# Score products and products with v on one ring of PSUM banks, with joined visits and two casts on other engines

## The chip, the cores and the metric

The program runs on one core of a Trainium2 chip. The metric is the device time of one execution in microseconds. A core has TensorE (PE, matrix products), VectorE (DVE), ScalarE (ACT), GpSimd (POOL) and SyncE (SP, which here only issues DMAs). Each engine works through its own queue in order; they meet through semaphores. TensorE writes its products to PSUM, eight banks of 2 KB per partition.

## The reference

Attention over 4 batches, 12 heads, 448 positions and 64 dimensions a head, with the heads mixed before and after the softmax, and two feed-forward layers behind it:

```python
scores = scale * np.matmul(q, k.transpose(0, 1, 3, 2))
scores = np.einsum('bhij,hg->bgij', scores, w_pre)
scores = scores - np.max(scores, axis=-1, keepdims=True)
attn = np.exp(scores)
attn = attn / (np.sum(attn, axis=-1, keepdims=True) + 1e-09)
attn = np.einsum('bhij,hg->bgij', attn, w_post)
out = np.matmul(attn, v)
# x: (1792, 768), all heads of a position in one row
h = x @ w_in;  x = (h * np.cos(h)) @ w_out
g = x @ w_gate;  y = (g / (1 + np.exp(-g)) * (x @ w_val)) @ w_out2
```

## The kernel before, in words

**Chunks and blocks.** The query positions of a batch are cut into four chunks of 12, 12, 11 and 10 blocks (`CH`); a block is ten positions with all twelve heads, 120 rows. 180 blocks in all, numbered through. The main loop (L438) runs over steps i, and in step i the stages of several blocks are issued: the score mix `premix` of block i, `rowmax` and `expo` of block i - 1, `den` of i - 2, `rec` and `norm_hi` of i - 3, `norm_lo` of i - 4, the post mix `post` of i - 6, `at_hi` and `at_lo` of i - 7 (lags, L336). What a step issues, and in which order, is set by the tuple `order` (L389): each engine's queue is that order restricted to its own work.

**A block's path.** `premix` (L220, TensorE, tile psm) mixes the heads of the scores x by `w_pre` into one of two banks. `rowmax` (L225, VectorE) takes the row maximum, `expo` (L233, ScalarE) the exponential and its row sum; both read the bank, which is free after `expo`. `den` and `rec` (L240, L244, VectorE) form the reciprocal. `norm_hi` (L249, GpSimd) and `norm_lo` (L256, VectorE) write the normalised rows as a sum of two fp16 parts. `post` (L269 to L271, twelve small products, TensorE, tile psa, two banks) mixes the heads again and transposes; `at_hi` (L282, ScalarE) and `at_lo` (L290, VectorE) write the result as two fp16 parts and free the bank.

**Score products.** The scores of a chunk are made while the chunk before is worked on. `qk` (L195, TensorE, tile pss) handles one head pair m of six: six products, three for each of two heads, with keys and queries as sums of a high and a low part. It takes two banks of the pool ps_s, which has two. `spread` (L211, ScalarE) copies a head's bank to a staging tile s (five of them) and issues, on SyncE's queue, the DMA that spreads it over x (L213). `QK_STEPS` gives the step of each head pair after the chunk's start; its two spreads stand one step later. The first mix of the next chunk needs all twelve spreads.

**Products with v.** `pv` (L302, TensorE, tile psv) handles one head pair: 24 products of 64 columns of weights. Three pairs share one bank of the pool ps_v, which also has two banks; `pv_out` (L319 ScalarE, L320 VectorE) empties it one step after the third. `PV_STEPS` gives the steps, counted from the end of the chunk, by the length of the chunk that follows. The small products of `pow2_b` and `w_sum_all` take banks of ps_v as well.

**Loads.** `dma_q` (L128) loads a chunk's queries seven steps before the chunk in front of theirs starts; `hi_q` (L132, VectorE, two halves) casts the high part and `lo_q` (L136, GpSimd) subtracts. `dma_k`, `hi_k` (L113, ScalarE) and `lo_k` (L117, GpSimd) do the same for the next batch's keys during the third chunk. `dma_v` (L140) loads a quarter of v, 112 positions; `split_v` scales it in place (L176, ScalarE), casts the high part (L179, VectorE) and subtracts in two halves (L182, GpSimd), over four steps that start two steps behind the load. Raw tiles of v have three buffers; all loads stand in SyncE's queue.

**Behind the attention.** The feed-forward part starts with the last chunk's early pieces and has its own loop; its lines are L732 to L734 (first products), L777 to L779 (second ones).

Of the kernel before, what the change touches and what calls it, by code (L numbers as in the profile page):

```python
# [7 lines left out]
F32 = mybir.dt.float32  # L8
# [9 lines left out]
SB = bass.MemoryType.SB  # L18
# [5 lines left out]
COFF = (0, 120, 240, 350)  # L24
CREAL = (120, 120, 110, 98)
FIRST = 4
QK_STEPS = {12: (0, 1, 3, 5, 7, 8), 11: (0, 4, 5, 6, 7, 8), 10: (0, 2, 3, 5, 6, 7)}
PV_STEPS = {11: (13, 13, 13, 15, 17, 17), 12: (11, 11, 11, 13, 15, 17), 10: (10, 10, 10, 14, 16, 16)}
SM = 1.0 / 8.0
INV2PI = 0.15915494309189535  # L30
TWOPI = 6.28318500518799
# [9 lines left out]
def attention(ctx, tc, qT, kT, vN, mix, xs, ff):  # L41
    nc = tc.nc
    scores = ExitStack()
# [7 lines left out]
    p_k = pool("a_k", 7, SB, scores, "right")  # L51
    p_kr = pool("a_kr", 3, SB, scores, "right")
    p_q = pool("a_q", 3, SB, scores, "right")
    p_s = pool("a_s", 5, SB, scores, "right")
    ps_s = pool("ps_s", 2, PSUM, scores, "right")
    p_vr = pool("a_vr", 3, SB, scores, "right")
    p_x = ff.p_x
# [8 lines left out]
    mixed = ExitStack()  # L66
    ps_m = pool("ps_m", 2, PSUM, mixed)

    ones = const.tile([128, 128], F32, name="ones")
    nc.vector.memset(ones, 1.0)  # L70
    nc.vector.tensor_copy(ff.ones, ones)
# [7 lines left out]
        return diag  # L79

    def pow2_b(diag, n, name):
        ps = ps_v.tile([128, 512], F32, tag="pv", name=f"psp_{name}")
        nc.tensor.matmul(ps[:, :n], ones[:n, :], diag[:n, :n], start=True, stop=True)
        return ps

# [10 lines left out]
        nc.vector.tensor_scalar(p[:, 1:2], p[:, 1:2], 8.0, None, op0=ALU.mult)  # L96
        return p

    ff.ps_sum = lambda name: ps_v.tile([128, 512], F32, tag="pv", name=name)
    ktiles, qtiles, vtiles, vscale = {}, {}, {}, {}  # L100
    raws = {}

# [24 lines left out]
        for s in parts:  # L127
            nc.sync.dma_start(raws["q", b, c][:, s], src[:, s])  # L128

    def hi_q(b, c, e, copy=nc.vector.tensor_copy):  # L130
        s = slice(3 * e, 3 * e + 3)
        copy(qtiles[b, c][0][:, s], raws["q", b, c][:, s])  # L132

# [36 lines left out]
    def split_v(b, jc, part):  # L170

        r = raws["v", "r", b, jc]
        rv = r.rearrange("p (m e d) -> p m e d", e=2, d=D)
        by = vscale[b][:112, 1:2]
        if part == 0:
            nc.scalar.activation(r, r, AF.Copy, scale=by)  # L176
        elif part == 1:
            t = vtiles[b, jc] = p_v.tile([112, 6, 2, 2, D], F16, tag="v", name=f"v_{b}_{jc}")
            nc.vector.tensor_copy(t[:, :, :, 0], rv)  # L179
        else:  # L180
            t, m = vtiles[b, jc], slice(3 * part - 6, 3 * part - 3)
            nc.gpsimd.tensor_tensor(t[:, m, :, 1], rv[:, m], t[:, m, :, 0], op=ALU.subtract)  # L182

    X, SP, SMALL, PM, E, EHL, PA, AT, PV = ({} for _ in range(9))

    def qk(b, c, m, places=((ps_s, "s"),)):

        n = 10 * CH[c]
        for e in range(2):
            pool, tag = places[(2 * m + e) % len(places)]  # L190
            SP[b, c, 2 * m + e] = pool.tile([128, 512], F32, tag=tag, name=f"pss_{b}_{c}_{2 * m + e}")
        for i, (zq, zk) in enumerate(((0, 0), (1, 0), (0, 1))):
            for e in range(2):
                r = slice(64 * e, 64 * e + 64)
                nc.tensor.matmul(  # L195
                    SP[b, c, 2 * m + e][:n, :S], qtiles[b, c][zq][r, m, :n], ktiles[b, m][zk][r],
                    start=(i == 0), stop=(i == 2),
                )
# [93 lines left out]
    def pv(b, c, m):  # L292


        n = 10 * CH[c]
        if m % 3 == 0:
            PV[b, c, m // 3] = ps_v.tile([128, 4, 128], F32, tag="pv", name=f"psv_{b}_{c}_{m}")
        ps = PV[b, c, m // 3]
        prods = [(jc, zv, za) for jc in range(4) for zv, za in ((0, 0), (0, 1), (1, 0))]
        for i, (jc, zv, za) in enumerate(prods):  # L300
            for e in range(2):
                nc.tensor.matmul(  # L302
                    ps[64 * e:64 * e + 64, m % 3, :n].rearrange("p (k i) -> p k i", i=10),
                    vtiles[b, jc][:, m, e, zv], AT[b, c][za][:, :, jc * H + 2 * m + e],
                    start=(i == 0), stop=(i == len(prods) - 1),
                )
# [24 lines left out]
    def at(i, fn, *a):  # L331
        plan.setdefault((i, fn.__name__), []).append((fn, a))

    first = {bc: blocks.index((*bc, 0)) for bc in chunks}
    for i, blk in enumerate(blocks):
        for fn, lag in ((premix, 0), (rowmax, 1), (expo, 1), (den, 2), (rec, 3), (norm_hi, 3),  # L336
                        (norm_lo, 4), (post, 6), (at_hi, 7), (at_lo, 7)):
            at(i + lag, fn, *blk)
    for ci, (b, c) in enumerate(chunks):
        n, s0 = CH[c], first[b, c]  # L340
        if ci + 1 < len(chunks):
            nb, ncn = chunks[ci + 1]
            for m in range(6):
                i = s0 + QK_STEPS[n][m]
                at(i, qk, nb, ncn, m)
                for e in range(2):
                    at(i + 1, spread, nb, ncn, 2 * m + e)
            if ci:
                at(s0 - 7, dma_q, nb, ncn)
                for e in range(2):  # L350
                    at(s0 - 2 + e, hi_q, nb, ncn, e)
                    at(s0 - 1 + e, lo_q, nb, ncn, e)
        if c == 2 and b + 1 < B:
            for m in range(6):
                i = s0 + 1 + 14 * m // 6
                at(i - 1, dma_k, b + 1, m)
                at(i + 2, hi_k, b + 1, m)
                at(i + 3, lo_k, b + 1, m)
        if c == 0:
            if b == 0:  # L360
                for part in range(3):
                    at(4 + part, scale_v, 0, part)
            if b + 1 < B:
                for part in range(3):
                    at(first[b, 3] + 7 + part, scale_v, b + 1, part)
            for jc in range(4):
                if b == 0:
                    if jc == 3:
                        at(1, dma_v, 0, jc, "m")
                    at(jc, max_v, 0, jc)  # L370
                v0 = s0 + 4 * jc + 5
                at(v0, dma_v, b, jc, "r")
                for part in range(4):
                    at(v0 + 2 + part, split_v, b, jc, part)
                if b + 1 < B:
                    i = first[b, 3]
                    at(i + jc, dma_v, b + 1, jc, "m")
                    at(i + jc + 2, max_v, b + 1, jc)
# [6 lines left out]

    for i, fn, *a in ff.early_plan(first[B - 1, 3]):
        at(i, fn, *a)

    order = (  # L389
        "rec", "pv_out", "pv", "post", "at_hi", "l1_part", "rowmax", "dma_v", "at_lo", "w_sum",  # L390
        "w_sum_all", "w_unit", "w_bits", "hidden", "den", "max_v", "scale_v", "hi_k", "dma_q",
        "lo_q", "spread", "split_v", "dma_k", "w_dma", "x_load", "load_next", "new_scale", "hi_q",
        "w_max", "w_shift", "w_split", "expo", "norm_hi", "premix", "qk", "lo_k", "norm_lo",
    )


    with tc.manual_schedule():
        vec, act, pl = nc.vector, nc.scalar, nc.gpsimd
# [39 lines left out]
        for i in range(-1, NB + 24):  # L438
            if i == first[B - 1, 3]:
                scores.close()  # L440
                ff.open_early()
            if i == NB + 1:
                mixed.close()
                ff.open_ps()
            for kind in order:
                for fn, a in plan.pop((i, kind), []):
                    fn(*a)
    assert not plan
# [529 lines left out]
```

## Time and profile before

| | |
|---|---|
| three runs | 1461.84, 1462.12, 1464.26 us; median 1462.12 |
| the profiled execution | 1462.24 us; span of its instructions 1460.4 us |
| TensorE | busy 1408.3 us, 96% of the span |
| VectorE | busy 1068.1 us, 73% |
| ScalarE | busy 646.3 us, 44% |
| GpSimd | busy 494.4 us, 34% |
| mean granted TensorE clock | 0.987 |

In the chain that ended last, followed back from the last instruction, TensorE has 76% of the span, VectorE 15%, ScalarE 4%, DMA transfers 3%. The busy shares are means over two very different parts, attention and feed-forward, so they are read by stretches. Matrix products are pipelined and overlap in the records: for TensorE the distance from one start to the next says more than an instruction's own duration, and in the rows below an "x6" is the first start and the whole length of six products.

### The profile page before, as it was taken

Reading aid. Unit: us, or ns where it says so; the run is one execution under the profiler, and the core shown is the slowest. Engines: PE = TensorE matmul, PEld = TensorE weight load, DVE = VectorE, ACT = ScalarE, POOL = GpSimd, SP = SyncE. Lnnn points to the kernel's source line nnn. Section 1 sums busy time; section 2 is a strip of 40 time slices with the busy share of each in tenths; the row PEclk is TensorE's granted clock in tenths of the full one; section 3 lists DMA queues with packets and bytes.
Section 4 is the critical chain, followed back from the end, with each engine's and each line's share of the span. In section 5 each row is a group of like instructions: output and inputs, shape, how many; then the busy total and the mean of one; then the engine's idle time right before and its main releaser. Section 6 shows DMA issues by size and latency. Waiting matters only on the chain.

```text
span 1460.4 us, 27063 instructions
## 1 busy us (share of the span) xinstructions
PE 1408.3 (96%) x10330; PEld 940.7 (64%) x10330; DVE 1068.1 (73%) x2310; ACT 646.3 (44%) x1374; POOL 494.4 (34%) x522
## 2 busy tenths in 40 slices
PE   6999999999999899999999999989999999999999
PEld 2556666656665566767676766656666666666666
DVE  5888989888988667878888878786355656565523
ACT  3777877877865353333333332444422223222210
POOL 2553553553532233323333332332223223222210
PEclk9999999999999999999999999999999999999999
DMA  6555555555546112121212221021112212211013
GB/s 203 147 155 152 154 157 157 149 156 149 156 140 226 44 55 77 54 66 54 77 54 66 65 65 44 22 65 55 55 44 66 66 44 69 62 55 33 1 38 114
DMA packets 102264, 131.77 MB, mean 90 GB/s; under 512 B 29848, under 2 KB 88696, under 8 KB 102136
## 3 DMA queue, kind: packets, MB, share of 16 engines
q1 hardware_dynamic: 101296, 128.77, 29.8%
q8 instruction: 81, 1.33, 0.4%
q10 hardware_dynamic: 840, 1.29, 0.3%
q14 instruction: 47, 0.39, 0.1%
HBM read 80.95 MB, written 10.37 MB: 63 GB/s over the span
## 4 chain that ended last, share of the span: by engine, by line
PE 76%; DVE 15%; ACT 4%; DMA 3%; issue 2%; SPq 0%; POOL 0%; ACTq 0%; DVEq 0%; POOLq 0%
PE ph L732 10%; PE ph L734 10%; PE ph L733 10%; PE psm L220 9%; PE py L777 7%; PE py L778 7%; PE py L779 7%; PE pss L195 5%; PE psv L302 4%; PE psa L269 3%; PE psa L270 2%; PE psa L271 2%; DVE acc L783 2%; DVE r L750 2%; DVE r L753 2%
## 5 line engine op out<-in xcount | busy, mean ns | idle before, releaser
L732 PE MATMUL ph<-x,h_i 128*128 128x448 f16 x960 | 339.4, 354 | 0.0
L733 PE MATMUL ph<-x,h_i 128*128 128x448 f16 x960 | 338.9, 353 | 0.0
L734 PE MATMUL ph<-x,l_i 128*128 128x448 f16 x960 | 338.9, 353 | 0.0
L762 POOL TENSOR_TENSOR gl<-r,gh 128x448 fp32r<-128x448 f32 x112 | 131.6, 1175 | 411.4 <-ACT gh L761 406.1
L777 PE MATMUL py<-gh,h_o 128*128 128x448 f32 x672 | 257.8, 384 | 11.5 <-DVE acc L783 6.2
L778 PE MATMUL py<-gl,h_o 128*128 128x448 f32 x672 | 245.5, 365 | 0.0
L779 PE MATMUL py<-gh,l_o 128*128 128x448 f32 x672 | 245.2, 365 | 0.1
L783 DVE TENSOR_TENSOR acc<-py,acc 128x448 f32<-128x448 f32 x288 | 174.4, 619 | 64.2 <-PE py L779 60.3
L220 PE MATMUL psm<-x,wpre_sb 120*120 120x448 f32 x360 | 181.1, 586 | 17.8 <-DMA x<-s 7.1
L249 POOL TENSOR_SCALAR eh<-e,sm 120x448 f16<-120x448 f32 x180 | 115.0, 639 | 183.8 <-DVE sm L244 113.9
L732 PEld LDWEIGHTS <-h_i 128*128 128x128 f16 x960 | 93.9, 98 | 92.4 <-issue 10.6
L777 PEld LDWEIGHTS py<-gh,h_o 128*128 128x128 f32 x672 | 127.3, 189 | 37.1 <-DVE acc L783 16.9
L734 PEld LDWEIGHTS <-l_i 128*128 128x128 f16 x960 | 94.0, 98 | 87.9 <-issue 0.4
L733 PEld LDWEIGHTS <-h_i 128*128 128x128 f16 x960 | 94.2, 98 | 82.0 <-issue 0.2
L225 DVE TENSOR_REDUCE sm<-psm 120x1 f32<-120x448 f32 x180 | 110.6, 615 | 41.7 <-PE psm L220 40.2
L233 ACT ACTIVATE e<-psm,sm 120x448 f32<-120x448 f32 x180 | 115.7, 643 | 56.9 <-DVE sm L225 55.1
L606 POOL TENSOR_TENSOR l_i<-f_i,h_i 128x384 f16<-128x384 f32 x80 | 81.3, 1016 | 174.9 <-ACT h_i L605 174.7
L760 DVE SCALAR_TENSOR_TENSOR r<-ph,by_i,r 128x448 f32<-128x448 f32 x48 | 32.8, 684 | 146.5 <-PE ph L734 115.8
L269 PE MATMUL psa<-wpost,eh 120*112 120x120 f16 x720 | 131.8, 226 | 4.9 <-DVE at L290 2.3
L779 PEld LDWEIGHTS py<-gh,l_o 128*128 128x128 f32 x672 | 127.0, 189 | 10.3 <-POOL l_o L606 1.3
L778 PEld LDWEIGHTS py<-gl,h_o 128*128 128x128 f32 x672 | 127.4, 190 | 7.5
L761 ACT CAST gh<-r 128x448 fp32r<-128x448 f32 x112 | 63.5, 567 | 155.0 <-DVE r L760 117.8
(105 smaller groups left out, 2451.3 us busy)
## 6 DMA issues: line engine op xcount, KB each, us to landing
r_o<-in_w_out SPq DMA_DIRECT2D x56, 384.0 KB
x<-s SPq DMA_DIRECT2D x84, 210.0 KB
r_i<-in_w_in SPq DMA_DIRECT2D x32, 384.0 KB
x<-s SPq DMA_DIRECT2D x48, 192.5 KB
r_i<-in_w_gate SPq DMA_DIRECT2D x24, 384.0 KB
r_i<-in_w_val SPq DMA_DIRECT2D x24, 384.0 KB
x<-s SPq DMA_DIRECT2D x48, 175.0 KB
qr<-in_qT SPq DMA_DIRECT2D x15, 360.0 KB
```

Of the source, the lines that this page charges most:

```text
L220: nc.tensor.matmul(ps[:120, :S], wpre_sb, X[b, c][:120, k], start=True, stop=True)
L233: nc.scalar.activation(e, PM.pop((b, c, k))[:120, :S], AF.Exp, bias=sm[:, 0:1], scale=1.0, accum_out=sm[:, 1:2])
L249: nc.gpsimd.tensor_scalar(eh, E[b, c, k], sm[:, 3:4], 1.0, op0=ALU.mult, op1=ALU.mult)
L269: nc.tensor.matmul(o, eh[:, j], wpost_sb[0], start=True, stop=False)
L732: nc.tensor.matmul(ps, wh, xh, start=(kk == 0), stop=False)
L733: nc.tensor.matmul(ps, wh, xl, start=False, stop=False)
L734: nc.tensor.matmul(ps, wl, xh, start=False, stop=(kk == 5))
L762: nc.gpsimd.tensor_tensor(gl, r, f(gh), op=ALU.subtract)
L777: nc.tensor.matmul(ps, wh, gh[:, e], start=(e == 0), stop=False)
L778: nc.tensor.matmul(ps, wh, gl[:, e], start=False, stop=False)
L779: nc.tensor.matmul(ps, wl, gh[:, e], start=False, stop=(e == 1))
L783: nc.vector.tensor_tensor(acc, ps, acc, op=ALU.add)
```

## The change

The constants: `QK_STEPS`, `PV_STEPS`, the steps of the loads and the order within a step are new; lags stand in a tuple, where `rec` moves from lag 3 to lag 2.

```diff
-QK_STEPS = {12: (0, 1, 3, 5, 7, 8), 11: (0, 4, 5, 6, 7, 8), 10: (0, 2, 3, 5, 6, 7)}
-PV_STEPS = {11: (13, 13, 13, 15, 17, 17), 12: (11, 11, 11, 13, 15, 17), 10: (10, 10, 10, 14, 16, 16)}
+LAGS = (0, 1, 1, 2, 2, 3, 4, 6, 7, 7)
+QK_STEPS = {12: (1, 1, 3, 3, 7, 7), 11: (1, 1, 3, 3, 7, 8), 10: (1, 1, 3, 3, 5, 6)}
+PV_STEPS = {12: (9, 9, 11, 17, 17, 17), 11: (10, 10, 10, 15, 15, 15), 10: (7, 9, 9, 15, 15, 15)}
+SECOND = 2
+Q_STEPS = (-11, -5, 0)
+K_STEPS = (3, 4, 6, 8, 10, 12)
+V_STEPS = (0, 3, 6, 9)
+SPLIT_STEPS = (3, 5, 6, 7)
+ORDER = (
+    "at_hi", "l1_part", "rowmax", "post", "dma_v", "lo_q", "premix", "den", "dma_k", "w_dma",
+    "x_load", "load_next", "new_scale", "split_v", "hi_k", "spread", "norm_hi", "max_v", "at_lo",
+    "w_sum", "w_sum_all", "w_unit", "w_bits", "hidden", "lo_k", "qk", "hi_q", "pv", "scale_v",
+    "rec", "norm_lo", "pv_out", "w_max", "w_shift", "w_split", "expo", "dma_q",
+)
-    p_s = pool("a_s", 5, SB, scores, "right")
+    p_s = pool("a_s", 6, SB, scores, "right")
+    banks = []
+
+    def bank(name):
+
+        second = len(banks) % 4 > 1 or "closed" in banks
+        banks.append(name)
+        pool, tag = (ps_v, "pv") if second else (ps_s, "s")
+        return pool.tile([128, 512], F32, tag=tag, name=name)
-        ps = ps_v.tile([128, 512], F32, tag="pv", name=f"psp_{name}")
+        ps = bank(f"psp_{name}")
-    ff.ps_sum = lambda name: ps_v.tile([128, 512], F32, tag="pv", name=name)
+    ff.ps_sum = bank
-    def hi_q(b, c, e, copy=nc.vector.tensor_copy):
+    def hi_q(b, c, e, copy=nc.scalar.copy):
-            nc.vector.tensor_copy(t[:, :, :, 0], rv)
+            nc.gpsimd.tensor_copy(t[:, :, :, 0], rv)
-    def qk(b, c, m, places=((ps_s, "s"),)):
+    def qk(b, c, m, places=()):
...
+                SP[b, c, 2 * m + e] = bank(name)
-            PV[b, c, m // 3] = ps_v.tile([128, 4, 128], F32, tag="pv", name=f"psv_{b}_{c}_{m}")
+            PV[b, c, m // 3] = bank(f"psv_{b}_{c}_{m}").rearrange("p (g i) -> p g i", g=4)
+                late = m and QK_STEPS[n][m - 1] == QK_STEPS[n][m]
                 for e in range(2):
-                    at(i + 1, spread, nb, ncn, 2 * m + e)
+                    at(i + (SECOND if late else 1), spread, nb, ncn, 2 * m + e)
-                at(s0 - 7, dma_q, nb, ncn)
+                at(s0 + Q_STEPS[0], dma_q, nb, ncn)
                 for e in range(2):
-                    at(s0 - 2 + e, hi_q, nb, ncn, e)
-                    at(s0 - 1 + e, lo_q, nb, ncn, e)
+                    at(s0 + Q_STEPS[1] + e, hi_q, nb, ncn, e)
+                    at(s0 + Q_STEPS[2] + e, lo_q, nb, ncn, e)
-                i = s0 + 1 + 14 * m // 6
+                i = s0 + K_STEPS[m]
-                v0 = s0 + 4 * jc + 5
+                v0 = s0 + V_STEPS[jc] if b else s0 + 2 * jc + 5
-                    at(v0 + 2 + part, split_v, b, jc, part)
+                    at(v0 + SPLIT_STEPS[part], split_v, b, jc, part)
```

The order before was:

```python
    order = (
        "rec", "pv_out", "pv", "post", "at_hi", "l1_part", "rowmax", "dma_v", "at_lo", "w_sum",
        "w_sum_all", "w_unit", "w_bits", "hidden", "den", "max_v", "scale_v", "hi_k", "dma_q",
        "lo_q", "spread", "split_v", "dma_k", "w_dma", "x_load", "load_next", "new_scale", "hi_q",
        "w_max", "w_shift", "w_split", "expo", "norm_hi", "premix", "qk", "lo_k", "norm_lo",
    )
```

`bank` hands out the two banks of ps_s and the two of ps_v in turn, to score products, products with v and the small sums alike; once the score pools are closed, at the start of the last chunk, it gives those of ps_v alone.

## Rows read from the trace of the kernel before

**Rows 1.** Busy time by stretch (us; instructions in brackets), then granted TensorE clock, DMA share, GB/s

```profile
0.00:53.30 53.30, 37.01 (x184) 19.46 (x185) 35.21 (x88) 25.13 (x55) 18.02 (x24) 0.94 0.65 193
53.30:431.40 378.10, 368.98 (x4582) 238.26 (x4583) 338.16 (x891) 287.73 (x700) 191.29 (x232) 0.99 0.52 149
431.40:493.20 61.80, 50.25 (x718) 34.06 (x717) 47.86 (x116) 28.81 (x63) 15.96 (x20) 0.91 0.56 179
493.20:1460.40 967.20, 952.06 (x4847) 648.97 (x4847) 646.84 (x1218) 304.65 (x559) 269.17 (x247) 1.00 0.19 56
```

**Rows 2.** Timeline of TensorE, 83.5 to 92.8 us: start, us, engine, line, operation, tiles, count

```profile
83.51 0.97 PE L220 MATMUL psm<-x,wpre_sb 120*120 120x448 f32 x2
...
84.40 0.83 PE L302 MATMUL psv<-at,v 112*64 112x120 f16 x24
...
85.83 0.97 PE L220 MATMUL psm<-x,wpre_sb 120*120 120x448 f32 x2
...
87.27 0.97 PE L220 MATMUL psm<-x,wpre_sb 120*120 120x448 f32 x2
...
88.17 0.85 PE L195 MATMUL pss<-k,q 64*100 64x448 f32 x6
...
88.95 0.83 PE L302 MATMUL psv<-at,v 112*64 112x120 f16 x24
...
90.38 0.97 PE L220 MATMUL psm<-x,wpre_sb 120*120 120x448 f32 x2
...
91.28 0.85 PE L195 MATMUL pss<-k,q 64*100 64x448 f32 x6
...
92.74 0.59 PE L220 MATMUL psm<-x,wpre_sb 120*120 120x448 f32 x1
```

**Rows 3.** The same timeline, at the first score mix of each batch's fourth chunk

```profile
106.07 1.48 PE L220 MATMUL psm<-x,wpre_sb 120*120 120x448 f32 x2 [3.12 <-DMA x<-s]
...
107.48 1.47 PE L195 MATMUL pss<-k,q 64*120 64x448 f32 x6
...
110.00 0.97 PE L220 MATMUL psm<-x,wpre_sb 120*120 120x448 f32 x2
...
214.74 0.98 PE L220 MATMUL psm<-x,wpre_sb 120*120 120x448 f32 x2 [1.93 <-ACT at L282]
...
324.56 1.51 PE L220 MATMUL psm<-x,wpre_sb 120*120 120x448 f32 x2 [2.27 <-DMA kr<-in_kT]
...
435.03 1.82 PE L220 MATMUL psm<-x,wpre_sb 120*120 120x448 f32 x2 [2.82 <-issue]
```

**Rows 4.** Busy time by stretch, two stretches behind such a chunk's first score mix

```profile
106.60:109.60 3.00, 3.00 (x15) 1.51 (x14) 1.92 (x5) 1.18 (x3) 0.00 (x0) 0.50 0.45 120
434.20:440.60 6.40, 5.57 (x38) 3.35 (x40) 2.84 (x7) 1.39 (x4) 1.07 (x2) 0.50 1.03 369
```

**Rows 5.** The chain that ended last, 98 to 110 us: start, us, what

```profile
100.67 5.31 DMA x<-s
```

**Rows 6.** Timeline of TensorE at the start: two visits of score products without other work between

```profile
14.25 2.60 PE L195 MATMUL pss<-k,q 64*120 64x448 f32 x12 [0.52 <-ACT s L211]
```

**Rows 7.** Timeline of TensorE: three head pairs of products with v in one visit

```profile
74.82 2.10 PE L302 MATMUL psv<-at,v 112*64 112x120 f16 x72
```

**Rows 8.** Groups of lines, shapes apart, 53.3 to 431.4 us: busy us, mean ns, idle before

```profile
L249 POOL TENSOR_SCALAR eh<-e,sm 120x448 f16<-120x448 f32 x158 | 100.5, 636 | 147.2 <-DVE sm L244 94.3 <-PE psa L271 14.8 <-ACT e L233 11.1
...
L182 POOL TENSOR_TENSOR v<-vr,v 112x384 f16<-112x384 f32 x30 | 37.3, 1245 | 22.2 <-DVE v L179 15.8 <-ACT s L211 3.9 <-ACT e L233 2.4
...
L136 POOL TENSOR_TENSOR q<-qr,q 128x360 fp32r<-128x360 f32 x26 | 34.3, 1320 | 16.5 <-DVE q L132 16.5
...
L132 DVE CAST q<-qr 128x360 fp32r<-128x360 f32 x26 | 10.3, 398 | 0.0
...
L179 DVE CAST v<-vr 112x768 f16<-112x768 f32 x15 | 8.3, 551 | 0.0
```

**Rows 9.** The queries' cast line: durations min/median/max in ns on ScalarE

```profile
L132 ACT CAST q<-qr x2: 491/492/494, 3.8 to 6.0; 128x360 fp32r<-128x360 f32 x2
```

More of the change, by code (lines that the diff above doesn't have):

```diff
@@ L184, in attention @@
     X, SP, SMALL, PM, E, EHL, PA, AT, PV = ({} for _ in range(9))
-    def qk(b, c, m, places=((ps_s, "s"),)):
+    def qk(b, c, m, places=()):
         n = 10 * CH[c]
         for e in range(2):
-            pool, tag = places[(2 * m + e) % len(places)]
-            SP[b, c, 2 * m + e] = pool.tile([128, 512], F32, tag=tag, name=f"pss_{b}_{c}_{2 * m + e}")
+            name = f"pss_{b}_{c}_{2 * m + e}"
+            if places:
+                pool, tag = places[(2 * m + e) % len(places)]
+                SP[b, c, 2 * m + e] = pool.tile([128, 512], F32, tag=tag, name=name)
+            else:
+                SP[b, c, 2 * m + e] = bank(name)
         for i, (zq, zk) in enumerate(((0, 0), (1, 0), (0, 1))):
@@ L335, in attention @@
     for i, blk in enumerate(blocks):
-        for fn, lag in ((premix, 0), (rowmax, 1), (expo, 1), (den, 2), (rec, 3), (norm_hi, 3),
-                        (norm_lo, 4), (post, 6), (at_hi, 7), (at_lo, 7)):
+        for fn, lag in zip(
+            (premix, rowmax, expo, den, rec, norm_hi, norm_lo, post, at_hi, at_lo), LAGS
+        ):
             at(i + lag, fn, *blk)
@@ L387, in attention @@
         at(i, fn, *a)
[L389 to L394, printed above, removed]
     with tc.manual_schedule():
@@ L440, in attention @@
                 scores.close()
+                banks.append("closed")
                 ff.open_early()
@@ L444, in attention @@
                 ff.open_ps()
-            for kind in order:
+            for kind in ORDER:
                 for fn, a in plan.pop((i, kind), []):
```

## The prediction, made before the change was run

> **What bounds the kernel now.** I read the busy times by stretch first. The feed-forward part behind 493 us isn't touched by the change [rows 1]; what it can move is the attention part, and of that the stretch from 53.3 to 431.4 us above all. There TensorE is busy 369.0 of 378.1 us, VectorE 338.2, ScalarE 287.7, GpSimd 191.3 [rows 1]: TensorE sets the pace, VectorE is close behind. The timeline of TensorE is read next, by the starts of the score mixes (psm), one per step. A plain step (mix, post mix) takes 87.27 - 85.83 = 1.44 us. A step with one visit of score products (pss) takes 92.74 - 90.38 = 2.36, so a visit adds 0.92. One head pair with v (psv) adds 85.83 - 83.51 - 1.44 = 0.88. Both kinds in a row add 90.38 - 87.27 - 1.44 = 1.67 instead of 1.80 [rows 2]. No idle time stands in these rows: what shortens TensorE's own work here shortens the stretch, if the others follow.
>
> The second thing to see is where TensorE does stand still: at the first mix of the fourth chunk of each batch, for 3.12, 1.93, 2.27 and 2.82 us [rows 3]. The chain names a spread transfer of x that takes 5.31 us [rows 5]. After each such gap the granted clock is 0.50, 1.2 of 2.4 GHz [rows 4], and the step that follows takes 110.00 - 106.07 = 3.93 us [rows 3] instead of 2.36 [rows 2].
>
> **Visits of score products.** Six visits a chunk become three (next to a 12-block chunk) or four. In the stretch at stake 35 second pairs join a first one: nine in first chunks of batches 1 to 3, twelve in second chunks, eight in third, six in fourth chunks; three more lie in the first chunk of all, which waits for loads, and count nothing. The trace has one place with two pairs in a row, at the start: 2.60 us for twelve products [rows 6], where six at the low clock take 1.47 [rows 3]. So the second pair costs 1.13 at the low clock, 0.57 at the high one. It cost 0.92 alone; a merge saves 0.35, together 12.3 us. The other end, if the second pair cost what a visit takes from its first product to the next kind, 88.95 - 88.17 = 0.78 [rows 2], is a merge worth 0.92 - 0.78 = 0.14, together 4.9. I take 0.35, since that row shows the very sequence.
>
> **Visits of products with v.** Four visits a chunk become three after first and fourth chunks, three become two after second ones: 11 merges outside the tail. Three pairs take 2.10 [rows 7], one 0.83 [rows 2], so a joined pair costs 0.64 and saves 0.88 - 0.64 = 0.24: 2.7 us. Against it: by the two step tables, 23 visits with v now follow directly on score products, and none will; that shared switch was worth 1.80 - 1.67 = 0.13, so 3.0 us are lost. Sum of the merges: 12.3 + 2.7 - 3.0 = 12.0 us.
>
> **The stall at the fourth chunk.** Last spreads still go out in step 9 of the third chunk, two steps ahead of the first mix. Two things change. Step 10 now holds three pairs of the second chunk with v: it takes 1.44 + 0.88 + 2.10 - 0.83 = 3.6 us instead of 1.44, so 2.1 us more lie between. And steps 5 to 9 now issue ten spreads of 175 KB (100 rows of 448 float32); after the change steps 8 and 9 issue four, with the other eight out by step 5: about 1 MB less stands in the queues ahead, which at the 149 GB/s of the stretch [rows 1] is 7 us of transfer, at the 193 of the start 5 us. Each exceeds the longest gap of 3.12. I count the four gaps as gone: 10.1 us, and behind three of them 3.93 - 2.36 = 1.57 us of low clock, 4.7. Behind the fourth the clock is low for 6.4 us [rows 4], which costs 3.2; half of it I leave in, because VectorE has the weights' scales to do there: 1.6. Sum 16.4 us.
>
> **Casts that change engines.** VectorE loses the queries' casts (10.3 us) and v's (8.3) [rows 8]: 18.6 us. Now nothing waits for that time, so it is priced at nothing by itself; it is the cover for the merges. Over the 158 steps VectorE's load falls from 338.2 to 319.6, 2.02 a step, against 2.94 (1.44 + 0.92 + 0.57) + 1.44 for a doubled step and a plain one, 2.19 each: it still fits, by 0.17 a step. ScalarE gains 26 casts of 0.49 [rows 9], 12.8 us: 300.5, or 1.90 a step, hidden under the same 2.19.
>
> GpSimd gains v's cast, 768 elements. Its one-input row takes 0.636 for 448, so 1.09; its subtraction takes 1.245 for half the tile, so 2.49 for the whole at worst [rows 8]. I take 1.09: one input, narrower output. In the twelve steps that hold a batch's splits GpSimd then does 12 x 0.64 + 4 x (1.09 + 2.49) + 2 x 1.32 [rows 8] = 24.6 us against 12 x 2.19 = 26.3: hidden. The price at 2.49 is among the rivals.
>
> **Loads and order.** v's raw loads (112 rows of 768 float32, 336 KB) go out up to eight steps earlier and get three steps, not two, before ScalarE's scaling, which stands in front of its copies; queries' loads go four steps earlier; keys' loads now stand ahead of a step's spreads on SyncE. In batch 0 the fourth v load, at step 11, must wait for the first tile's split at step 12; behind it on SyncE stands nothing until step 13, but ScalarE's scaling of step 14 waits for it, and all copies and exponentials stand behind that. TensorE's cyclic order (post mix, score mix, score products, v) stays. The reciprocal comes one step earlier, so GpSimd, which idles 94.3 us for it [rows 8], starts sooner. In the second of two doubled visits (steps 1 and 3) the last pair needs banks that ScalarE empties in step 3 itself: a new wait, with the next post mix behind it. For all this I add 3 us; the ends are 0 and 12 (three gaps of a fourth-chunk kind, about 4 us with their low clock, in other places).
>
> **Sum.** The profiled execution took 1462.24 us (span 1460.4), within 0.2 us of the median 1462.12. 1462.2 - 12.0 - 16.4 + 3 = 1437 us. What a measurement can tell from no change is about 0.2%, 3 us.
>
> **Rivals.**
> - *VectorE sets the pace.* Then the stretch gets no shorter than VectorE's own load does: 1462.2 - 18.6 = 1444. For it: 338.2 busy of 378.1. Against it: the 0.17 us a step left over.
> - *GpSimd falls behind in v's splits*, with a cast of 2.49. A batch's twelve steps then hold 30.2 us of its work, 3.9 more than they last, of which the step between norm_hi and norm_lo covers 2.2: 1.7 in three batches. In batch 0, where the casts stand two steps apart, nine steps hold 9 x 0.64 + 4 x 4.98 + 2 x 1.32 = 28.3 against 19.7, 6.4 after the same cover. Norm_lo on VectorE waits for it: 1437 + 5.1 + 6.4 = 1448. For it: the subtraction is that slow. Against it: one input.
> The Trainium skill, GPSIMD Engine Reference, Engine selection, takes this side: elementwise work belongs on VectorE, GpSimd being about half as fast with two inputs, though roughly at line rate with one. By half of VectorE's speed the cast would take 2 x 0.55 = 1.1 us (an estimate) and the sum would stay 1437; no row here shows a cast on GpSimd.
> - *The visits don't join*, so the change doesn't do what it says: the second pair waits for its two banks, each merge gives back its 0.35, and 1437 + 12.3 = 1449. For it: steps 1 and 3 are doubled with one step between, and ScalarE copies two tiles a step. Against it: by the plan only the last pair of step 3 meets banks that are emptied in the same step.
> - *The fourth chunk still waits.* The landing is late whatever is queued: 1437 + 16.4 = 1453. For it: the last spread goes out at the same step. Against it: 2.1 us more work between.
> - *Both of the last two*: 1437 + 28.7 = 1466, on the border of slower.
> - *Slower: x is late at the head of the other chunks too.* Place: the 11 other heads behind 53 us, above all second chunks, where v's fourth load now goes out at step 9 ahead of the last spreads of the same step. Price: (10.1 + 4.7 + 1.6) / 4 = 4.1 us a head, so 11 x 4.1 = 45, in all 1482. It decides from 25 / 4.1, six heads, on. For it: the transfer of 5.31 us; DMA at 52% of its time already. Against it: those heads have three steps, not two, and hardly stall now.
>
> **Chances.** My forecast 0.48 (own range 1429 to 1445), VectorE 0.09, GpSimd 0.05, visits not joined 0.14, fourth chunk 0.10, the last two together 0.07 (0.04 of it within 0.2%), slower heads 0.07. So faster 0.86, same 0.04, slower 0.10. The range runs from 1427 (no new waits, 3; the fourth gap's whole low clock, 1.6; the stretch's other idle time, 9.1 - 7.3 = 1.8; and 3 of the 16 us that TensorE idles in the first 53 [rows 1]) to 1454, which takes in the first four rivals.
>
> **What would show it.** Right: twelve score products in a row, about 1.35 us between the mixes' neighbours; no idle time over 1 us at the four first mixes, and no clock of 0.50 behind them; 53 to 431 us shrinking to about 350; the casts as 0.49 on ScalarE and about 1.1 on GpSimd. Wrong: a gap inside a doubled visit that ends on a copy of ScalarE; psm waiting for x at second chunks; VectorE without idle time while TensorE waits for it; post mixes waiting for eh on GpSimd in the steps of the splits.

## The result, and the profile after

The changed kernel takes 1438.04 us (median of four runs, 1435.51 to 1440.35), the kernel before 1461.98 (four runs, 1461.32 to 1464.26): a ratio of 0.983, 95% interval 0.981 to 0.985, 24 us faster. 1437 was forecast. The profiled execution took 1440.35 us, the slowest of the four; against the 1462.24 of the one before that is 21.9 less, and it is these 21.9 that the traces have to account for.

In the changed file the score mix is L245, score products L220, post mix L294 to L296, products with v L327; the queries' cast is L153 and subtraction L157, v's scaling L197, its cast L200, its subtraction L203; `norm_hi` is L274, `norm_lo` L281.

Busy times by stretch, cut at the first mix of the second chunk, the first mix of the last chunk and the first product of the second feed-forward step, and two short stretches for the clock; columns as in [rows 1]. The second stretch of [rows 1] ends 3.6 us ahead of the last chunk's first mix (435.03), so the first line here gives the kernel before up to that mix; the others are the changed kernel's:

```profile
53.31:435.03 381.72, 369.79 (x4595) 238.96 (x4595) 340.55 (x898) 289.46 (x703) 192.56 (x234) 0.99 0.52 150
...
0.00:53.70 53.70, 36.82 (x184) 20.91 (x185) 33.00 (x82) 26.79 (x59) 19.31 (x25) 0.94 0.66 192
53.70:414.60 360.90, 355.07 (x4671) 241.67 (x4669) 327.43 (x859) 295.25 (x730) 220.03 (x249) 1.00 0.55 157
414.60:471.30 56.70, 46.86 (x633) 31.38 (x633) 46.59 (x107) 26.88 (x58) 17.33 (x20) 0.92 0.57 184
471.30:1438.60 967.30, 951.62 (x4850) 648.80 (x4847) 645.71 (x1218) 304.77 (x559) 268.96 (x247) 1.00 0.19 56
45.80:52.40 6.60, 6.03 (x29) 4.08 (x30) 4.72 (x14) 5.45 (x15) 4.40 (x6) 0.50 0.59 181
106.60:109.60 3.00, 2.59 (x18) 1.52 (x20) 1.57 (x5) 1.26 (x4) 0.42 (x2) 1.00 1.11 266
```

The feed-forward part keeps its 967 us. Up to the second chunk the kernel loses 0.4 (53.3 to 53.7). The 158 steps that follow go from 381.7 us (53.31 to 435.03) to 360.8 (53.74 to 414.58), 20.9 less. From the last chunk's first mix to the second products it is 56.7 where it was 58.2, 1.5 less. The two stretches don't hold quite the same work, though: three pairs of the last batch's second chunk with v (72 products) now stand in step 10 of the third chunk, ahead of the last chunk's first mix, where the kernel before has them behind it. At 3.60 - 1.43 = 2.17 us for three pairs, like for like the 158 steps gain 23.0 us and the part behind them loses 0.7. So all of it is where the prediction put it but for the last chunk, which gains nothing. Up to the same mix VectorE went down from 340.6 to 327.4 busy, 13.2 us where 18.6 us of casts left it; 319.6 was expected. TensorE is busy 355.1 of 360.9.

TensorE's timeline, in order of time: one mix behind step 8 of the first chunk, the first mixes of the four fourth chunks, and between them a plain step and a doubled one:

```profile
46.37 1.85 PE L245 MATMUL psm<-x,wpre_sb 120*120 120x448 f32 x2 [2.46 <-ACT e L258]
...
107.01 0.98 PE L245 MATMUL psm<-x,wpre_sb 120*120 120x448 f32 x2 [1.27 <-ACT k L134]
...
183.98 0.97 PE L245 MATMUL psm<-x,wpre_sb 120*120 120x448 f32 x2
...
185.42 0.97 PE L245 MATMUL psm<-x,wpre_sb 120*120 120x448 f32 x2
186.31 1.47 PE L220 MATMUL pss<-k,q 64*100 64x448 f32 x12
...
188.38 0.97 PE L245 MATMUL psm<-x,wpre_sb 120*120 120x448 f32 x2
...
210.17 0.98 PE L245 MATMUL psm<-x,wpre_sb 120*120 120x448 f32 x2 [1.00 <-ACT at L307]
...
312.88 0.98 PE L245 MATMUL psm<-x,wpre_sb 120*120 120x448 f32 x2 [1.09 <-DMA x<-s]
...
414.58 0.98 PE L245 MATMUL psm<-x,wpre_sb 120*120 120x448 f32 x2 [0.39 <-ACT e L258]
```

Three things are to be seen. Twelve score products stand in a row and take 1.47 us, where six took 0.85 [rows 2]: the second pair costs 0.62, and the step 188.38 - 185.42 = 2.96. The plain step is still 1.44. The four waits of [rows 3] have shrunk from 10.1 us to 3.75 but not gone, and no low clock follows on them: 106.6 to 109.6 stands at 1.00, where it was 0.50 [rows 4]. And there is a stall that the kernel before has not in this place: 2.46 us in front of 46.37, with 6.6 us at 0.50 behind it. The kernel before has its low clock of the first chunk from 34.8 us on; the clock of the whole first stretch is 0.94 in both.

### The profile page after: what moved, and what is told of

The parts are those of the page before. It is cut to its first block, busy times and chain, and to the rows that moved or that the text cites. A ratio compares the mean times of both kernels' runs of the same rounds, so it can differ in the third digit from the quotient of the medians.

```text
span 1438.6 us, 27003 instructions
## 1 busy us (share of the span) xinstructions
PE 1390.4 (97%) x10330; PEld 942.8 (66%) x10330; DVE 1052.7 (73%) x2264; ACT 653.7 (45%) x1404; POOL 525.6 (37%) x538
## 4 chain that ended last, share of the span: by engine, by line
PE 77%; DVE 16%; ACT 4%; issue 1%; DMA 1%; ACTq 0%; SPq 0%; DVEq 0%
PE ph L752 11%; PE ph L754 11%; PE ph L753 11%; PE psm L245 8%; PE py L797 8%; PE py L798 7%; PE py L799 7%; PE pss L220 4%; PE psv L327 3%; PE psa L294 3%; PE psa L295 2%; PE psa L296 2%; DVE r L770 2%; DVE r L773 2%; DVE k L769 2%
## 5 line engine op out<-in xcount | busy, mean ns | idle before, releaser
L274 POOL TENSOR_SCALAR eh<-e,sm 120x448 f16<-120x448 f32 x180 | 151.4, 841 | 175.0 <-ACT e L258 51.3
L245 PE MATMUL psm<-x,wpre_sb 120*120 120x448 f32 x360 | 180.5, 585 | 11.7 <-DMA x<-s 4.4
L797 PEld LDWEIGHTS py<-gh,h_o 128*128 128x128 f32 x672 | 127.2, 189 | 36.6 <-DVE acc L803 15.7
L250 DVE TENSOR_REDUCE sm<-psm 120x1 f32<-120x448 f32 x180 | 111.3, 618 | 36.6 <-PE psm L245 35.8
L294 PE MATMUL psa<-wpost,eh 120*112 120x120 f16 x720 | 130.1, 224 | 2.9 <-DVE at L315 1.3
```

What stands on the lines that cost most here:

```text
L245: nc.tensor.matmul(ps[:120, :S], wpre_sb, X[b, c][:120, k], start=True, stop=True)
L274: nc.gpsimd.tensor_scalar(eh, E[b, c, k], sm[:, 3:4], 1.0, op0=ALU.mult, op1=ALU.mult)
L294: nc.tensor.matmul(o, eh[:, j], wpost_sb[0], start=True, stop=False)
L797: nc.tensor.matmul(ps, wh, gh[:, e], start=(e == 0), stop=False)
```

## The experiments

All kernels of one group ran on the same chip beside the kernel before; ratios are to that. Where kernels of two groups are compared, it is by their ratios.

### Are joined visits worth time, and how much?

```diff
-QK_STEPS = {12: (1, 1, 3, 3, 7, 7), 11: (1, 1, 3, 3, 7, 8), 10: (1, 1, 3, 3, 5, 6)}
+QK_STEPS = {12: (1, 2, 3, 4, 7, 8), 11: (1, 2, 3, 4, 7, 8), 10: (1, 2, 3, 4, 5, 6)}
```

> The changed kernel with every second head pair of score products one step later, as a visit of its own; spreads stay in the steps they have. My theory: TensorE sets the pace and a joined visit saves the difference of steps, 2 x 2.36 against 2.97 + 1.43, that is 0.32 us, 35 times in the stretch from 53 us on: about 11 us slower than the changed kernel, 1449 us, and no step of 2.97 us left. Rival: VectorE sets the pace, so joining pays nothing: within 3 us of the changed kernel's 1438.

1447.79 us, ratio 0.992 (0.990 to 0.994) where the changed kernel has 0.983: 0.0086 of 1462, 12.6 us slower than the changed kernel. Its stretch of 158 steps, and four mixes of its timeline:

```profile
51.70:422.60 370.90, 365.30 (x4666) 235.87 (x4667) 332.66 (x859) 296.36 (x730) 221.30 (x250) 1.00 0.54 153
```

```profile
183.67 0.97 PE L245 MATMUL psm<-x,wpre_sb 120*120 120x448 f32 x2
185.10 0.97 PE L245 MATMUL psm<-x,wpre_sb 120*120 120x448 f32 x2
...
187.45 0.97 PE L245 MATMUL psm<-x,wpre_sb 120*120 120x448 f32 x2
...
189.81 0.97 PE L245 MATMUL psm<-x,wpre_sb 120*120 120x448 f32 x2
```

370.9 us against 360.9: 10.0 us in the trace for 35 merges, 0.29 each, other waits included; two steps of 2.36 take the place of one of 2.96 and one of 1.44, 0.32 more. The theory of the joined visits holds, and VectorE as the pace of the kernel is out: were it so, parting the visits would have cost nothing. What a visit pays once is what it costs beyond its products, 0.92 - 0.62 = 0.30. The Trainium skill, TensorEngine Tiling (Array Packing), Tiling Modes, says that changing the tiling mode drains TensorE. Score products use half of the rows (64) and mixes nearly all (120), and the 0.30 fits that, though no run here parts a drain from other costs of a visit.

### What kept the fourth chunk waiting?

Two edits look at it from two sides. In the changed kernel the work that fills the time of landing is taken away:

```diff
-PV_STEPS = {12: (9, 9, 11, 17, 17, 17), 11: (10, 10, 10, 15, 15, 15), 10: (7, 9, 9, 15, 15, 15)}
+PV_STEPS = {12: (9, 9, 11, 17, 17, 17), 11: (6, 6, 6, 15, 15, 15), 10: (7, 9, 9, 15, 15, 15)}
```

> The changed kernel with the three head pairs with v of step 10 of the third chunk in step 6 instead, so that steps 9 and 10 are plain. My theory: those pairs fill the time in which the last spreads land; without them each first mix of a fourth chunk waits some 2.1 us longer (2.9 to 3.4 us instead of 0.4 to 1.3), falls to the low clock and loses about 1.5 us more: 4 x 3.6, about 14 us slower, 1452. Rival: the shorter queue of spreads alone removed the stall: waits as in the changed kernel, 1438.

1450.47 us (1444.36 to 1453.94, the profiled one the fastest), ratio 0.994 (0.991 to 0.996): 15 us slower than the changed kernel. The four first mixes of fourth chunks:

```profile
104.05 0.98 PE L245 MATMUL psm<-x,wpre_sb 120*120 120x448 f32 x2 [2.96 <-ACT k L134]
...
208.73 1.82 PE L245 MATMUL psm<-x,wpre_sb 120*120 120x448 f32 x2 [3.04 <-DMA vm<-in_vN]
...
315.68 0.98 PE L245 MATMUL psm<-x,wpre_sb 120*120 120x448 f32 x2 [2.53 <-DMA x<-s]
...
419.60 1.74 PE L245 MATMUL psm<-x,wpre_sb 120*120 120x448 f32 x2 [2.46 <-ACT at L307]
```

The waits sum to 10.99 us, as long as before the change (10.14), though ten spreads no longer stand in a row in front of them. So in the changed kernel it is the three pairs with v in step 10 that cover the landing, and the shorter queue alone would not have done it. Two of the four mixes (1.82 and 1.74 us long) run at the low clock, the others don't. The trace is of the fastest execution, 6 us under the median, and shows 7.2 us more of waits than the changed kernel's; the other five have a lower granted clock (0.989 to 0.991, against 0.993), so part of the 15 us is probably low clock that this trace lacks; how much is not shown.

How long the last spread takes can be read from SyncE. Its issue at the first of the four heads in the changed kernel, in this one and in the next one:

```profile
101.40 0.76 SPq L238 DMA_DIRECT2D x<-s  x1
...
98.75 0.76 SPq L238 DMA_DIRECT2D x<-s  x1
...
100.36 0.76 SPq L213 DMA_DIRECT2D x<-s  x1
```

From there to the first mix it is 5.61 us in the changed kernel, 5.30 in this one, and 5.40 in the kernel before (100.67 [rows 5] to 106.07); over the four heads 4.7 to 5.6, 4.8 to 5.4 and 4.2 to 5.4. The shorter queue has not made the landing sooner. In batches 0 to 2 a load of keys, which now goes out ahead of the last spread, may take back what the queue gives; batch 3 loads no keys, and there it is 4.83 us in this kernel and 5.10 in the one before.

In the kernel before, pairs 1 to 5 are made one or two steps earlier, so that the last spread goes out one step earlier:

```diff
-QK_STEPS = {12: (0, 1, 3, 5, 7, 8), 11: (0, 4, 5, 6, 7, 8), 10: (0, 2, 3, 5, 6, 7)}
+QK_STEPS = {12: (0, 1, 3, 5, 7, 8), 11: (0, 2, 4, 5, 6, 7), 10: (0, 2, 3, 5, 6, 7)}
```

> The kernel before with one thing changed: the third chunk's visits of score products in steps 0, 2, 4, 5, 6, 7 instead of 0, 4, 5, 6, 7, 8, so that its last spread goes out one step earlier. My theory: the four waits of 3.12, 1.93, 2.27 and 2.82 us and the low clock behind them go nearly whole, 13 to 16 us: 1446 to 1449 us. Rival: what is late is the transfer whatever is queued, or the stall moves to another place: less than 6 us gained, 1456 or more.

1451.28 us, ratio 0.994 (0.992 to 0.996): 8.6 us faster than the kernel before, between what the two theories said.

```profile
105.33 0.98 PE L220 MATMUL psm<-x,wpre_sb 120*120 120x448 f32 x2 [0.65 <-issue]
...
212.32 0.98 PE L220 MATMUL psm<-x,wpre_sb 120*120 120x448 f32 x2 [0.65 <-issue]
...
319.91 0.98 PE L220 MATMUL psm<-x,wpre_sb 120*120 120x448 f32 x2 [1.16 <-DMA vm<-in_vN]
...
427.02 0.98 PE L220 MATMUL psm<-x,wpre_sb 120*120 120x448 f32 x2 [0.97 <-issue]
```

The waits fall from 10.1 to 3.4 us and no mix here is longer than 0.98. From the last spread's issue to the first mix it is 5.0 to 5.5 us here too: the stall was the step in which the last spread goes out, and most of it can be mended without the ring. The step gives back 6.7 us of waiting. The steps behind the first three heads, which took 3.92, 3.56 and 3.92 us, take 2.39, another 4.2 us, and the two behind the fourth take 2.8 less. At the four heads that is 13.7 us, as expected, but the span of the profiled execution falls by 10.2 only (1460.4 to 1450.2) and the time by 8.6. One step that gives some back is the first of the second chunk, 3.91 us at the low clock where 2.37 is its work; the rest isn't accounted for.

### Did the casts on other engines matter?

Both casts back on VectorE, in the changed kernel:

```diff
-    def hi_q(b, c, e, copy=nc.scalar.copy):
+    def hi_q(b, c, e, copy=nc.vector.tensor_copy):
-            nc.gpsimd.tensor_copy(t[:, :, :, 0], rv)
+            nc.vector.tensor_copy(t[:, :, :, 0], rv)
```

> The changed kernel with both casts (queries' and v's high parts) on VectorE again. My theory: the moved 18.6 us are cover, not path, so the time stays within 4 us of 1438; in batch 0 it may even fall by 2 to 3 us, because the two norm_lo of 1.9 us that stand beside v's splits on GpSimd go back to 0.7. Rival: VectorE sets the pace of the changed kernel, and 18.6 us come back in good part: 1446 to 1457.

1438.62 us, ratio 0.985 (0.983 to 0.988): 0.002 above the changed kernel, 3 us, and the intervals overlap. Its stretch:

```profile
52.90:413.90 361.00, 356.83 (x4667) 241.59 (x4667) 341.18 (x898) 284.44 (x699) 215.84 (x233) 1.00 0.55 157
```

361.0 us with VectorE at 341.2 busy, 360.9 with 327.4: VectorE can be busy for 94.5% of the stretch and still not be what TensorE waits for. The casts are cover that wasn't needed. The 2 to 3 us that batch 0 might have gained did not come. And the other way round, the kernel before with the two casts alone moved (the same four lines, reversed):

> The kernel before with the two casts alone moved: queries' to ScalarE, v's to GpSimd. My theory: TensorE sets the pace there and VectorE's 18.6 us less are worth nothing by themselves: within 4 us of the kernel before, and every step keeps its length. Rival: VectorE sets the pace, at least in part: 8 to 18 us faster.

1465.02 us (11 runs), ratio 1.0022 (1.0009 to 1.0035): 3 us slower, not faster. Why VectorE was not relieved stands in its trace: first the stretch of 158 steps, then `norm_lo` (here L256), then a pair of instructions from its timeline.

```profile
54.15:436.97 382.82, 371.75 (x4594) 239.44 (x4595) 343.51 (x857) 298.91 (x730) 190.37 (x250) 0.98 0.52 149
```

```profile
L256 DVE SCALAR_TENSOR_TENSOR el<-e,sm,eh 120x448 f16<-120x448 f32 x159 | 129.0, 811 | 0.0
```

```profile
154.84 0.92 POOL L182 TENSOR_TENSOR v<-vr,v 112x384 f16<-112x384 f32 x1
155.11 1.13 DVE L256 SCALAR_TENSOR_TENSOR el<-e,sm,eh 120x448 f16<-120x448 f32 x1
```

VectorE lost 18.6 us of casts and is as busy as before: 343.5 where it was 340.6 over the same 158 steps. `norm_lo` has gone from 0.70 to 0.81 on average, 17.8 us in all, because 43 of them now take 1.1 to 1.4 instead of 0.7. In the pair shown, GpSimd's subtraction starts 0.27 us ahead, takes 0.92 instead of the 1.245 of [rows 8], and it is `norm_lo` that stretches, ending 0.48 after it. In the pairs shown here and below, the one that starts first runs at its own speed and the other waits.

### Is GpSimd slower in the changed kernel, or does it wait?

The changed kernel's groups of lines on GpSimd, VectorE and ScalarE in the 158 steps:

```profile
L274 POOL TENSOR_SCALAR eh<-e,sm 120x448 f16<-120x448 f32 x160 | 134.0, 838 | 140.9 <-ACT e L258 46.4 <-PE psa L296 29.4 <-DVE sm L269 24.4
L281 DVE SCALAR_TENSOR_TENSOR el<-e,sm,eh 120x448 f16<-120x448 f32 x159 | 112.2, 706 | 0.0
...
L203 POOL TENSOR_TENSOR v<-vr,v 112x384 f16<-112x384 f32 x30 | 29.8, 995 | 0.0
...
L153 ACT CAST q<-qr 128x360 fp32r<-128x360 f32 x26 | 13.3, 511 | 0.0
...
L200 POOL CAST v<-vr 112x768 f16<-112x768 f32 x14 | 11.9, 849 | 0.0
```

`norm_hi` takes 838 ns where it took 636, v's subtraction 995 where it took 1245 [rows 8]. The edit puts the reciprocal back where it was:

```diff
-LAGS = (0, 1, 1, 2, 2, 3, 4, 6, 7, 7)
+LAGS = (0, 1, 1, 2, 3, 3, 4, 6, 7, 7)
 ORDER = (
-    "at_hi", "l1_part", "rowmax", "post", "dma_v", "lo_q", "premix", "den", "dma_k", "w_dma",
+    "rec", "at_hi", "l1_part", "rowmax", "post", "dma_v", "lo_q", "premix", "den", "dma_k", "w_dma",
...
-    "rec", "norm_lo", "pv_out", "w_max", "w_shift", "w_split", "expo", "dma_q",
+    "norm_lo", "pv_out", "w_max", "w_shift", "w_split", "expo", "dma_q",
```

> The changed kernel with the reciprocal back at lag 3 and first in the order, as before the change. In the changed kernel norm_hi on GpSimd takes 841 ns on average instead of 636. My theory: it is not GpSimd's work that is slower; it now starts while norm_lo on VectorE, which reads two tiles of SBUF, is running, and waits for it. With the reciprocal late it starts beside rowmax and at_lo again and takes about 640 on average. The time changes by less than 4 us, since neither is waited for in the steady steps. Rival: GpSimd is slower for another reason (v's cast in its queue, transfers), and norm_hi stays above 800.

1435.96 us, ratio 0.983 (0.981 to 0.985): the same time. Its groups:

```profile
L281 DVE SCALAR_TENSOR_TENSOR el<-e,sm,eh 120x448 f16<-120x448 f32 x159 | 114.2, 718 | 1.1 <-POOL eh L274 0.8
L274 POOL TENSOR_SCALAR eh<-e,sm 120x448 f16<-120x448 f32 x159 | 110.2, 694 | 140.0 <-DVE sm L269 99.5 <-ACT e L258 12.8 <-PE pss L220 9.7
```

`norm_hi` falls to 694 on average, most of the way. GpSimd isn't slower at the work, it waits beside `norm_lo`, and where `norm_hi` stands free of it the wait moves elsewhere: v's subtraction goes from 995 to 1225 ns and the queries' from 1032 to 1331. The Trainium skill, SBUF — State Buffer, Who interferes with whom, has the rule: a VectorE instruction with two SBUF inputs contends with a GpSimd instruction that reads SBUF, since its second input comes through the read interface that the two engines share; that pair of ports is an exclusive lock, which the one that issues first holds for the whole instruction, while the other is blocked. `norm_lo`, with the exponentials and `norm_hi`'s result as inputs, is such a one, and the traces agree in both directions, with 0.2 to 0.5 us a meeting. The prediction looked only at how fast GpSimd is.

### What is left to gain?

Four kernels of one group; the first is the changed kernel unaltered.

> The changed kernel once more, as the measure for the three kernels beside it on the same chip: 0.983 of the kernel before. Both of its stalls should stand where the first profile has them: about 2.5 us and a low clock behind it near 43 us, and 0.4 to 1.3 us at each first mix of a fourth chunk. Were they chance, this profile lacks them.

1436.72 us (1434.94 to 1439.12), ratio 0.984 (0.982 to 0.986). Both stalls stand there again (a step of 4.72 us in the first chunk with the low clock from 44.4 us on, last steps of the third chunks of 4.74, 4.46, 5.35 and 4.12 us where 3.6 is their work). The second one is in every trace of the changed kernel and its variants but the two with the next edit, which is made against it. The first one is in part chance: the kernel with v's pairs in step 6 differs from the changed one only from the third chunk on, and in its trace ScalarE waits 0.38 us for the tile of v for which it waits 1.71 and 2.23 in the two of the changed kernel, no wait of TensorE there is over 1.3 us, and the clock from 44 to 51 us is 1.00:

```profile
40.36 0.94 ACT L197 ACTIVATE vr<-vr,p_v 112x768 f32<-112x768 f32 x1 [0.38 <-DMA vr<-in_vN]
```

```diff
-QK_STEPS = {12: (1, 1, 3, 3, 7, 7), 11: (1, 1, 3, 3, 7, 8), 10: (1, 1, 3, 3, 5, 6)}
+QK_STEPS = {12: (1, 1, 3, 3, 7, 7), 11: (1, 1, 3, 3, 6, 7), 10: (1, 1, 3, 3, 5, 6)}
```

> The changed kernel with the third chunk's last two visits of score products in steps 6 and 7 instead of 7 and 8. My theory: what is left of the stall at the fourth chunks (1.44, 1.17, 1.25 and 0.55 us over a step without one) is the landing of the last spread, and goes: 3 to 4.5 us faster than the changed kernel. Rival: TensorE gets there sooner but VectorE or ScalarE is then what it waits for: no gain over 1 us.

1434.62 us (1433.20 to 1435.55), ratio 0.982 (0.980 to 0.984): 2.1 us less by the medians; one of its five runs lies among the changed kernel's, and the intervals of the ratios overlap. The mixes of the third chunk's last steps and the first of the fourth:

```profile
98.59 0.97 PE L245 MATMUL psm<-x,wpre_sb 120*120 120x448 f32 x2
...
100.14 1.01 PE L245 MATMUL psm<-x,wpre_sb 120*120 120x448 f32 x2
...
102.03 0.97 PE L245 MATMUL psm<-x,wpre_sb 120*120 120x448 f32 x2
...
105.64 0.97 PE L245 MATMUL psm<-x,wpre_sb 120*120 120x448 f32 x2
```

The wait at 105.64 is gone, and the step in front of it is 3.61. But the two plain steps ahead take 1.55 and 1.89 instead of 1.44: 0.6 us is given back in each of three batches (0.2 in the last, which has no keys to cast), as the theory did not have it and the rival in part did. In these two steps ScalarE, with a copy of scores, exponentials, `at_hi` and a cast of keys, is the engine without idle time, busy 3.40 of 3.40 us:

```profile
98.60:102.00 3.40, 3.17 (x31) 1.94 (x30) 2.99 (x9) 3.40 (x9) 2.48 (x3) 1.00 0.51 134
```

```diff
-                v0 = s0 + V_STEPS[jc] if b else s0 + 2 * jc + 5
+                v0 = s0 + V_STEPS[jc] if b else s0 + 3 * jc + 4
-                    at(v0 + SPLIT_STEPS[part], split_v, b, jc, part)
+                    at(v0 + (SPLIT_STEPS if b else (4, 5, 6, 7))[part], split_v, b, jc, part)
```

> The changed kernel with batch 0's four raw loads of v in steps 4, 7, 10, 13 instead of 5, 7, 9, 11, each scaled four steps later, not three. My theory: ScalarE's wait of 1.7 us for the first of them (43 us), TensorE's low clock behind it and the two norm_lo of 1.9 us beside v's splits go: 4 to 7 us faster than the changed kernel. Rival: the start is bound by the spreads' transfers whatever v does, and the stall only moves: within 2 us.

1434.11 us (1432.66 to 1434.75), ratio 0.982 (0.980 to 0.984): 2.6 us less, not 4 to 7. All its runs lie under those of the changed kernel, though the intervals of the ratios overlap. In the changed kernel's timeline ScalarE waits for v's first tile, and further on VectorE's `norm_lo` stands between GpSimd's queue of splits:

```profile
43.51 0.93 ACT L197 ACTIVATE vr<-vr,p_v 112x768 f32<-112x768 f32 x1 [1.71 <-DMA vr<-in_vN]
...
54.22 0.94 POOL L157 TENSOR_TENSOR q<-qr,q 128x360 fp32r<-128x360 f32 x1
54.54 1.97 DVE L281 SCALAR_TENSOR_TENSOR el<-e,sm,eh 120x448 f16<-120x448 f32 x1
...
55.13 0.91 POOL L203 TENSOR_TENSOR v<-vr,v 112x384 f16<-112x384 f32 x1
```

With the edit ScalarE's row has no wait and the clock stays up, but `norm_lo` still meets the splits (41.82), and VectorE has no idle time left there:

```profile
40.56 0.93 ACT L197 ACTIVATE vr<-vr,p_v 112x768 f32<-112x768 f32 x1
...
41.82 1.65 DVE L281 SCALAR_TENSOR_TENSOR el<-e,sm,eh 120x448 f16<-120x448 f32 x1
```

```profile
45.00:52.00 7.00, 5.38 (x55) 3.43 (x53) 7.00 (x17) 5.04 (x13) 6.93 (x8) 1.00 0.76 224
```

VectorE is busy 7.00 of 7.00 us: at the end of the first chunk, with few score products and none with v, VectorE is the bound. That the rest of the expected gain went there is likely, but not shown. The first chunk ends at 50.43 us here; it ends at 50.40 in the kernel with v's pairs in step 6, whose loads are the changed kernel's, at 52.5 and 53.7 in the two traces of the changed kernel. So what the edit gives in this trace is no more than an execution without the late tile has anyway.

Both edits together:

> Both of the last two edits together. My theory: the two stalls lie in different places and their gains add, 7 to 11 us faster than the changed kernel, about 1429 us where that takes 1438. Rival: one of them gives nothing, and the sum is that of the other alone.

1433.85 us (1432.36 to 1434.36), ratio 0.982 (0.980 to 0.984). It has the lowest median of all kernels here, 28 us under the kernel before (1462.28 in this group), and every run of it lies under the lowest of the changed kernel; it is not told apart from either edit alone. But the gains do not add: 2.9 us against 2.1 and 2.6 alone. In its profile both stalls are gone and its stretch is 357.5 us (52.13 to 409.60) against 360.2 of the changed kernel beside it (52.52 to 412.76), but the first chunk ends at 52.1 where the edit alone had it at 50.4. Its clock is at 0.50 for 3.4 us from 36.6 us on. The kernel with the third chunk's edit alone, whose first chunk is the changed kernel's, looks the same there: 0.50 for 3.4 us from 35.5 us on, the first chunk ending at 52.4. So this late end needs neither edit; the start differs from one execution to the next, by up to 3.3 us (50.4 to 53.7) where the first chunks are the same.

## Why the prediction was right, point by point

1437 against 1438 is closer than the reasoning deserves. The forecast was a fall of 25.4 us in three terms, 12.0 + 16.4 - 3, and the traces have 21.9: the merges were put 1 us too high and the stall over 5, the new waits cost nothing net, and the median lies 2.3 under the profiled execution. That the visits join and that work ahead of the fourth chunk covers the landing is shown; that a shorter queue does is not borne out; and the nearness of the number is in part luck.

**The bound.** Right. TensorE sets the pace: parting the visits costs what their steps say, and 18.6 us more or less on VectorE cost 0.2% at most either way.

**Visits of score products: 12.3 us forecast, 10 to 12.6 measured.** The second pair took 0.62 us, not 0.57. A merge saved 0.32 by the steps (0.29 by the traces' stretches, 0.36 by the whole times), where 0.35 was forecast. The row at the low clock that gave 0.57 was the right one to lean on; the other end, 0.14 a merge, was far off. Merges of products with v and the lost neighbours weren't tried by themselves.

**The stall at the fourth chunk: 16.4 us forecast, about 11 came.** The waits fell by 6.4 us, not by 10.1, and the low clock behind three of them is gone; it was put at 4.7 and had cost 4.3, since one of the three steps took 3.56 and not 3.93. Behind the fourth the low clock is gone too, but in the same chunk the clock falls to 0.50 from 428.1 us on for 6.8 us, and like for like the part from the last chunk's first mix on got no shorter: of the 1.6 forecast there nothing came. The step that failed is "each exceeds the longest gap": the two effects, 2.1 us more work and some 5 us less transfer ahead, were both taken as whole. The run with v's pairs in step 6 shows that the shorter queue gives next to nothing (10.99 us of waits against 10.14, and 5.30 us from the last issue to the mix against 5.40), so that only the 2.1 us a head remained, 8.4 of the 10.1 at most.

**New waits: 3 us forecast.** The sum of the traces is -10.9 (merges at 0.32, with the 2.7 and 3.0 as forecast, which no run tests) - 10.7 (6.4 and 4.3) against the 21.9 that came, so no net loss is left. That is not because nothing new waits: by the starts of the 180 mixes, steps of the 158 lose about 4.4 us apart from the four heads, 2.3 of it in steps 2, 4, 5 and 6 of batch 0's second chunk (2.29, 1.96, 1.87 and 1.87 where 1.43 is the work). But the kernel before lost about 5.1 us in such small waits in other places, which the prediction did not count, and these are gone. The wait that was feared in the second of two doubled visits did not come: all 35 doubled steps take 2.96 to 3.09. Both places named are real: v's loads in batch 0, though at the first tile and not the fourth (1.71 us on ScalarE, 2.46 on TensorE, then 6.6 us at the low clock), and GpSimd's splits there, though not for the reason given: at 54.54 `norm_lo` and the splits hold each other off.

**Casts.** The price of nothing was right, its reason half wrong. VectorE's load was to fall by 18.6 us and fell by 13.2; GpSimd's cast took 0.82 to 0.85, not 1.09. By the estimate that the prediction makes from the Trainium skill, GPSIMD Engine Reference, Engine selection, it was to take 1.1, twice VectorE's 0.55; it took 1.5 times that. Outside batch 0 GpSimd did not fall behind. What the sums lacked is that `norm_lo` and GpSimd's instructions hold each other off, so a microsecond moved to GpSimd can come back as a wait on VectorE: nearly all of it did in the kernel before (17.8 of 18.6 us), 1.0 us in the changed one, where GpSimd's `norm_hi` waits instead.

**Rivals.** VectorE as the pace: out, except for some 7 us in the first chunk. Visits that don't join: out, no gap stands in the 1.47 us. The fourth chunk still waiting: true by a third. Late x at other heads: out, the first mixes of the second chunks wait 0.55 and 0.15 us in two batches, where it was 0.81 and 0.10.

## What to carry to other kernels

When a trace shows one engine without gaps, count how often it changes between kinds of work, and price a change by the smallest place where two visits already stand together: that one row gave this forecast its 12.3 us. When a stall is a landing, ask what work lies between the last issue and the first use, and put independent work there or issue earlier; either did more than a shorter queue. Cut the stretches of two traces at the same work, and count the instructions in them, before comparing. Before moving work from VectorE to GpSimd, look which of VectorE's instructions read two SBUF tiles at that moment: the load may come back as their wait.

## What the runs showed of the hardware that was not expected

`norm_lo` on VectorE, with two SBUF inputs, and GpSimd's instructions hold each other off, one instruction at a time. `norm_hi` takes 0.64 us on average in the kernel before [rows 8] and 0.90 when it starts 0.27 us behind a `norm_lo`, as here in the changed kernel's timeline; `norm_lo`, 0.66 there, takes 1.13 behind a subtraction, and 1.97 between two instructions of GpSimd that follow on each other.

```profile
186.62 0.66 DVE L281 SCALAR_TENSOR_TENSOR el<-e,sm,eh 120x448 f16<-120x448 f32 x1
...
186.89 0.90 POOL L274 TENSOR_SCALAR eh<-e,sm 120x448 f16<-120x448 f32 x1 [1.36 <-ACT e L258]
```

The one that comes second ends 0.5 us after the first (187.79 against 187.28 here), against the 0.64 of its work, so the two hardly overlap. VectorE's other large instructions, which read PSUM, kept 0.62 and 0.65 us on average, as in the kernel before.

The clock after a wait is not settled by its length: of the waits of 2.5 to 3.0 us in one trace (the run with v's pairs in step 6) two were followed by the low clock and two were not.
